# A written-out order of steps for linear attention with an expert layer, replaced by another one

## The chip, the cores and the metric

The kernel runs on one core of a Trainium2 chip. The metric is the device time of one execution in microseconds (us); the time given for a kernel is the median of its runs. The core has a matrix engine (PE, with PEld for its weight loads), a vector engine (DVE), a scalar engine (ACT), a general engine (POOL), and a queue (SP) that issues all transfers of this kernel. Each engine takes its instructions strictly in the order in which the program gave them, and waits where an operand is not there yet.

## The reference

The inputs are `q`, `k`, `v` with 8 batches, 8 heads, 576 rows and 64 columns, and the weights of a feed-forward layer. All are float32 or float64 as drawn; the feed-forward weights arrive as 64-bit words.

```python
q_s = softmax(q, axis=-1)              # over a head's 64 columns
k_s = softmax(k, axis=2)               # over the 576 rows
kv  = einsum('bhsd,bhse->bhde', k_s, v)
x   = einsum('bhsd,bhde->bhse', q_s, kv)     # -> 4608 x 512
h   = x @ w_in                         # 512 -> 1024
solu = h * softmax(h, axis=-1)
ln  = (solu - mean) / sqrt(var + 1e-06) * g_ln
out = ln @ w_out                       # 1024 -> 512, float32
```

## The kernel before

The 4608 rows are cut into 36 tiles of 128 rows: four tiles for each batch from its first 512 rows, and one for each pair of batches from the 64 rows that remain of each. The work is written as Python generators, one per piece of work, and each `yield` ends a step. The pieces are:

- `LK`, `LV`, `LQ`, `V` (batch number): transfers of keys, values, queries, and the copy of values into `vm` (L161 on ACT, L163 on DVE).
- `K` + batch: the softmax of the keys and their product with the values. DVE takes the largest over rows in parts (`khalf` L365, `ktop` L367 and L370), PE turns it (`turned` L341), DVE reduces it (`col` L344), PE spreads it (`wide` L348), ACT copies it (`kb` L351), POOL or DVE subtracts it (`km` L376, `kr` L381), ACT takes the exponential (L378, L383), and PE multiplies (`kv` L395, L400). The result goes, scaled, into `bd` (L422 to L426).
- `Q` + batch + a, b or c: the softmax of the queries (L443 largest, L445 subtraction, L447 exponential, L450 sum, L452, L454, L456 product, L161 or L163 cast into `qhl`, L461 the rest of the cast), and a transposing transfer (L484).
- `x` + tile: attention of one tile on PE (L529), brought into two float16 halves (`xT`, ACT L541, DVE L543).
- `h` + tile: 24 products of 512 columns into `h` (L566; the very first tile has 16 float32 ones, L558), and then the chain of the activation: largest (DVE L573), `nm` (ACT L575), exponential `e` (ACT L579), four small steps on POOL or DVE (L583, L586, L589, L592), the product (DVE L595), the mean `nmu` (ACT L597), two float16 halves `u` (ACT L600, DVE L602), a transposing transfer (L605), and the squares (ACT L609), which are the last to read `h`. There are two buffers for `h`, so that a tile's first product waits for the squares of the tile two places ahead of it.
- `o` + tile: 24 products into the output (L640), the eviction (ACT L650 or DVE L648), and the transfer out (L653).
- `w`, `W`, `y`, `Z`: loading and splitting of the two weight matrices; `S`: a scale; `R`: queries of the remaining rows; `P`: four warm-up products of no use (L696).

What sets the order is a string, `ORDER`. It names one piece after another; each name runs that piece up to its next `yield`. A suffix `.v` puts the step on DVE, where the step can choose its engine; without it the step goes to POOL or ACT, as the line says. `*2` repeats. So `ORDER` alone decides in which order each engine, and the transfer queue, gets its instructions, and which engine takes the optional ones:

```python
for item in order.split():
    item, _, times = item.partition("*")
    key, _, engine = item.partition(".")
    for _ in range(int(times or 1)):
        step(key, engine)
```

Of the kernel before, what the change touches and what calls it, by code (L numbers as in the profile page):

```python
# [23 lines left out]
    "LQ0*2 LK0 Q0a.v Q0a Q0b.v Q0a.v LK0 Q0c.v K0 LK0 w3 K0 w3 Q0c.v V00 K0 V03 Q0c.v Q0b K0 w0 P w0 "  # L24
    "Q0b.v w3 Q0a.v V00 K0 Q0b Q0a K0 K0.v Q0a K0 V03 V02.v K0 w3*2 Q0a.v LV0 V01 Q0b w0 K0.v P K0 V02 "
    "V01 P K0.v K0 w2 w0*2 Q0a K0.v K0 Q0b.v P K0 w0 Q0b K0 Q0c w2 K0 w2 K0 w1 w2 w1 LK1 K0*2 Q0b P K0 w2 "
    "Q0c w3 P w1*2 P K0*2 P K0*2 w1 w2 K0*2 w1 K1*2 x0 W LK1 x0 Q0c K1 W*2 h0 K1 V11 W V11 h0 K1 V12 y0 "
    "h0 Q0c.v W*4 h0.v W y0 W x1 y0 S0 K1 y1 W x1 y1 y0 h0.v V13.v K1 y1 y0 x1 LQ1 Q0c h0.v K1 h1 K1 h1.v "
    "h0 y1 y2 h1.v W LV2 V12 h0 h1.v x2 x3 y0 h0.v V13 y2 h0 h0.v h1 Q1a h0 h1.v K1 P V10 y1 y3 K1 x2 "
    "h0.v*2 Q1a x3 h0.v x2 Q1a h1 y2 K1 h1.v y1 K1 x3 h1.v*2 K1 h1 Q1a h2*2 V10.v h2 h1 Q1c K1 LG h2 "  # L30
    "Q1a*2 h1 h2*2 h1 LV1 y2 h2.v K1 h2.v K1 Q1a K1*2 h2 y3 P h2 Q1a.v y3 h1.v K1*2 LQ1 h1.v P h1.v y2 "
    "h2.v h2 K1 y2 Q1c h1 h3 K1*2 h2 y3 K1 h3*2 K1 h2 h3 y3 LK2 h3 K1 y3 K1 x5 h2 x4 h1.v Z x5*2 h2*2 h0 "
    "h0.v h0 h3.v h0.v Q1c.v Z*2 h1.v Z*2 h3 Z h5 Z h5 Z*2 o0.v Z h1 h2.v Z h5 Z*2 V22.v Z h2 Z LK2 h5.v "
    "h5 Z o0.v o0 h2 Z*3 h3*2 V21 o0 h3*3 LQ1 V22 Z o0 V21 Q1c o1 h5.v V23 o0 Q1c o1.v x4 S1 h3 R1.v R1 "
    "h3.v h5 h3 V23.v R1 h2.v K2 x4 o1.v o1*2 Q1c h3.v h3 h5*2 h4.v R1 K2 Q1c h4 V20.v Q1c.v h4.v K2 o0 "
    "h5 K2.v LQ2 h4 R1.v h3.v h5.v h3 h4 R1 K2 h5.v h4.v K2 o2 o1 h5.v o2.v o1.v h5.v K2.v*2 h4.v x6 x7 "
    "h5 h5.v K2.v x6 R1.v o2 h4.v h4 V32 h4.v h4 x6 h5 S1.v o2.v*2 R1 K2 h3.v K2 Q2a V20 K2.v h6.v h4 "
    "K2.v h4.v Q2c.v K2 h6 h6.v h6 h4.v h6 h6.v K2 h4.v h5.v x7 Q2a V33 K2.v o2 x8 Q2c h4 Q2a.v h6 K2 "
    "h4.v K2 x7 h7.v h3 h6.v Q2a h7 h6.v h4 K2.v Q2c h6.v h7.v h5 K2 Q2c Q2a LV3 o3.v V33 h7.v h5.v h6 "
    "h6.v o3.v h7 K2 K2.v Q2a h5 LK3 Q2a.v K2.v h4.v K2*2 K2.v h4 Q2c h7 K2 Q2a o3 K2.v h7 V32.v h7.v K3 "  # L40
    "h6.v o3 K3.v h6.v o3 h4.v o3.v K3 S2 o4.v x9 x10 h6.v o4 x9 S1 o4 K3 LK3 h7 x8 K3 h7 Q2c o4 h6.v "
    "h7.v*2 x9 o3 h6 x10 h6 h9 h7 K3 V31.v h7 K3.v h9.v*2 h7.v Q2c.v h9.v h7.v h9*2 o2 K3.v x10 h7.v K3 "
    "h6.v o4 h9 LQ3 h9 h10.v K3.v o5 h9.v h10 V30.v h9 Q2c.v h10.v h10 V31 h9.v LQ3 h9 h6 o4 h7 x8 h10 "
    "o5.v h6 h9.v h9*2 h10.v K3.v*2 h9 K3.v K3 h9.v o5 h7.v o5.v h10 Q3c o6 h10 h10.v h10 V30 h8.v K3.v "
    "h10.v Q3a o5.v h10 h10.v h8.v h7.v h8*2 K3.v Q3a LV4 Q3a.v o5.v K3 h10.v Q3c.v Q3a h10.v h10 x11 K3 "
    "x12 LK4 h8 x11 x12 h7 Q3a*2 x11 K3 h8 LQ3 o6.v h8 V41.v h8.v K3 h8 h8.v h10 K3 K3.v V43 h8 h8.v K3.v "
# [47 lines left out]
    "o33 h35*2 o31 o27 h35.v o28.v o27.v h34*2 o27*4 h34.v h35.v h34.v h34 h34.v o31 h35 h34 h35.v o30.v "  # L94
    "h34 o31 o33 o27 o30 o30.v*2 h34 o32.v o33 h35 o30.v o33 h35.v h35 o32 o28.v h35.v o30.v o31.v o32.v "
    "h35.v o32 h35 o31 h35 o32 h35 o32 h35 h35.v o32.v h35 h35.v o34 o35 o33 o34 o33 o34 o33.v o34 o34.v "
    "o34 o34.v o35.v*3 o35*2 o35.v*2 o35*5 "
)


# [660 lines left out]
```

## Time and profile before

| what | value |
|---|---|
| time, median of 3 runs | 473.68 us (472.71 to 475.24) |
| the profiled execution, its own time | 472.75 us |
| its span, first to last instruction | 471.0 us |
| PE busy | 443.1 us, 94% of the span |
| DVE, ACT, POOL busy | 350.5, 285.5, 196.1 us |

The page of the profile shows one execution. The share of an engine's busy time is an average over the whole span; the beginning, where weights and the first keys are loaded and prepared, differs from the long middle, where PE always has a tile to work on. A row of the trace gives start, duration (both in us), engine, line, operation, output <- input, and in brackets how long the engine stood idle ahead of it and what ended that.

### The profile page before, as it was taken

The page shows a single profiled execution, that of the slowest core. Times are in us where ns is not written, and L with a number is a line of the kernel's source. Part 1 is how long each engine was busy: PE and PEld are TensorE (multiplying, and loading weights), DVE is VectorE, ACT ScalarE, POOL GpSimd, SP SyncE. Part 2 cuts the span into 40 slices and gives each one's busy share as a digit, 9 for nine tenths or more (in the row PEclk, how much of TensorE's full clock was granted, in tenths as well). Part 3 has the DMA queues.
Part 4 walks back from the last instruction along what each step waited for, and adds up shares of the span by engine and source line. Part 5 has one row for each costly group of instructions (what it writes and reads, how often), then busy time and mean ns, then how long its engine had stood idle before and what let it go on. Part 6 is the DMA issues. An engine that isn't in the chain of part 4 may idle for free.

```text
span 471.0 us, 8293 instructions
## 1 busy us (share of the span) xinstructions
PE 443.1 (94%) x3142; PEld 221.2 (47%) x3142; DVE 350.5 (74%) x602; ACT 285.5 (61%) x473; POOL 196.1 (42%) x300
## 2 busy tenths in 40 slices
PE   1678989998999999999999999999999999999997
PEld 0333444455545444544454455444445444444444
DVE  4989999989989887788998888875856755554030
ACT  2688999668657674757576557644566545431231
POOL 4122974665434194941255357412353431221100
PEclk9989999999999999999999999999999999999999
DMA  8999968696695958299859944797222462515141
GB/s 271 267 273 344 244 143 200 131 236 162 125 211 116 250 133 226 73 209 216 191 150 208 227 101 81 167 276 169 69 67 53 106 134 47 123 34 111 47 129 49
DMA packets 159240, 74.99 MB, mean 159 GB/s; under 512 B 127840, under 2 KB 152672, under 8 KB 159200
## 3 DMA queue, kind: packets, MB, share of 16 engines
q1 hardware_dynamic: 159200, 74.47, 67.1%
q8 instruction: 24, 0.39, 0.3%
q14 instruction: 16, 0.13, 0.1%
HBM read 36.70 MB, written 9.44 MB: 98 GB/s over the span
## 4 chain that ended last, share of the span: by engine, by line
PE 68%; DVE 18%; DMA 5%; issue 3%; ACT 3%; POOL 1%; SPq 1%; DVEq 0%; ACTq 0%; POOLq 0%
PE o L640 32%; PE h L566 30%; PE kv L395 3%; DMA qm<-in_q_dram 2%; PE x L529 2%; DVE h L595 2%; DMA km<-in_k_dram 2%; DVE u L602 2%; DVE top L573 2%; DVE khalf L365 1%; DVE qnmx L443 1%; DVE wo L330 1%; DVE qsum L450 1%; DMA kr<-in_k_dram 1%; PE kv L400 1%
## 5 line engine op out<-in xcount | busy, mean ns | idle before, releaser
L640 PE MATMUL o<-wo,uT 128*128 128x512 f16 (+1 forms) x888 | 198.3, 373 | 0.3 <-ACT os L650 0.2
L566 PE MATMUL h<-wi,xT 128*128 128x512 f16 x840 | 194.0, 379 | 4.7 <-ACT e L609 4.0
L640 PEld LDWEIGHTS <-uT 128*128 128x128 f16 x888 | 86.1, 98 | 97.1 <-issue 0.7
L566 PEld LDWEIGHTS <-xT 128*128 128x128 f16 x840 | 81.6, 98 | 102.3 <-issue 5.7
L573 DVE TENSOR_REDUCE top<-h 128x1 f32<-128x1024 f32 x36 | 43.9, 1221 | 21.5 <-PE h L566 21.3
L602 DVE SCALAR_TENSOR_TENSOR u<-h,nmu,u 128x1024 f16<-128x1024 f32 x36 | 46.0, 1277 | 15.6 <-ACT u L600 15.5
L595 DVE SCALAR_TENSOR_TENSOR h<-h,ph,e 128x1024 f32<-128x1024 f32 x36 | 46.3, 1285 | 11.7 <-POOL ph L592 9.8
L609 ACT ACTIVATE e<-h,nmu 128x1024 f32<-128x1024 f32 x36 | 40.1, 1113 | 18.5 <-DVE u L602 18.4
L456 POOL TENSOR_TENSOR qm<-qm,qrec 128x1024 f32<-128x1024 f32 (+1 forms) x15 | 27.4, 1825 | 39.2 <-DVE qrec L454 30.8
L600 ACT ACTIVATE u<-h,nmu 128x1024 f16<-128x1024 f32 x36 | 40.0, 1112 | 1.0
L589 POOL TENSOR_TENSOR p<-pi,mone 128x1 f32<-128x1 f32 x36 | 24.2, 672 | 36.1 <-DVE pi L586 34.6
L579 ACT ACTIVATE e<-h,nm,hs 128x1024 f32<-128x1024 f32 x31 | 37.3, 1202 | 0.7
L597 ACT ACTIVATE nmu<-s 128x1 f32<-128x1 f32 x36 | 7.3, 202 | 46.2 <-DVE h L595 45.9
L575 ACT ACTIVATE nm<-top,hs 128x1 f32<-128x1 f32 x31 | 9.1, 293 | 40.5 <-DVE top L573 40.4
L650 ACT ACTIVATE os<-o,rr 128x512 f32<-128x512 f32 (+1 forms) x24 | 16.0, 665 | 26.3 <-PE o L640 23.7
L583 POOL TENSOR_SCALAR am<-nm 128x1 f32<-128x1 f32 x19 | 9.0, 471 | 50.0 <-ACT nm L575 49.9
L622 POOL TENSOR_TENSOR r<-var,mhalf 128x1 f32<-128x1 f32 x36 | 21.6, 599 | 17.1 <-DVE var L619 15.2
L543 DVE SCALAR_TENSOR_TENSOR xT<-x,xT 128x512 f16<-128x512 f32 x35 | 23.8, 681 | 2.4 <-ACT xT L541 2.4
L443 DVE TENSOR_REDUCE qnmx<-qm 128x16 f32<-128x1024 f32 (+1 forms) x17 | 19.4, 1149 | 6.9 <-DMA qm<-in_q_dram 6.9
L447 ACT ACTIVATE qm<-qm 128x1024 f32<-128x1024 f32 (+1 forms) x17 | 17.0, 1005 | 11.7 <-POOL qm L445 7.7
L541 ACT ACTIVATE xT<-x 128x512 f16<-128x512 f32 x35 | 20.0, 594 | 6.5 <-PE x L529 6.5
L376 POOL TENSOR_TENSOR km<-km,kb 128x1024 f32<-128x1024 f32 x8 | 18.9, 2360 | 6.4 <-ACT kb L351 6.3
(138 smaller groups left out, 556.9 us busy)
## 6 DMA issues: line engine op xcount, KB each, us to landing
v<-in_v_dram SPq DMA_DIRECT2D x32, 256.0 KB, 4.1
out_dram<-os SPq DMA_DIRECT2D x31, 256.0 KB, 3.3
km<-in_k_dram SPq DMA_DIRECT2D x7, 1024.0 KB, 6.5
qm<-in_q_dram SPq DMA_DIRECT2D x7, 1024.0 KB, 7.0
w_in<-in_moe_w_in_dram SPq DMA_DIRECT2D x8, 512.0 KB, 7.1
w_out<-in_moe_w_out_dram SPq DMA_DIRECT2D x8, 512.0 KB, 4.9
out_dram<-os SPq DMA_DIRECT2D x10, 128.0 KB, 2.4
qm<-in_q_dram SPq DMA_DIRECT2D x2, 512.0 KB, 4.3
```

Source lines behind the costliest of these rows:

```text
L443: nc.vector.tensor_reduce(shaped(nmx), x, axis=AX.X, op=ALU.max, negate=True)
L456: on(nc.gpsimd).tensor_tensor(x, x, wide(rec), op=ALU.mult)
L543: nc.vector.scalar_tensor_tensor(xT[:, 1], acc, 1.0 / QS, xT[:, 0], op0=ALU.mult, op1=ALU.subtract)
L566: nc.tensor.matmul(h[:, ns], xT[:, t, kc], wi[:, s, kc, ns], start=(i == 0), stop=(i == len(terms) - 1))
L573: nc.vector.tensor_reduce(top, h, axis=AX.X, op=ALU.max, negate=True)
L579: nc.scalar.activation(e, h, AF.Exp, bias=nm, scale=hs, accum_out=z)
L589: nc.gpsimd.tensor_tensor(p, pi, mone, op=ALU.pow)
L595: nc.vector.scalar_tensor_tensor(h, h, ph, e, op0=ALU.mult, op1=ALU.mult, accum_out=s1)
L600: nc.scalar.activation(u[:, 0], h, AF.Identity, bias=nmu)
L602: nc.vector.scalar_tensor_tensor(u[:, 1], h, nmu, u[:, 0], op0=ALU.add, op1=ALU.subtract)
L609: nc.scalar.activation(e, h, AF.Square, bias=nmu, accum_out=s2)
L640: nc.tensor.matmul(o, uT[:, j, f], wo[:, s, f, cols], start=(f == 0 and j == 0 and s == 0), stop=(f == NF - 1 and j == 1))
```

## The change

Only the string `ORDER` is another one. It has the same 1725 steps, each as often as before, among them 11 warm-up steps `P`; the steps stand in another order, and other ones of them have the suffix `.v`. Its first line before and after:

```diff
-    "LQ0*2 LK0 Q0a.v Q0a Q0b.v Q0a.v LK0 Q0c.v K0 LK0 w3 K0 w3 Q0c.v V00 K0 V03 Q0c.v Q0b K0 w0 P w0 "
+    "LQ0*2 Q0a*2 LK0*3 Q0b.v Q0c.v Q0a.v Q0b V03 K0.v w3 Q0a w3 K0 Q0a.v Q0a K0*2 Q0b V03 Q0c.v*2 V00 w0 "
```

PE gets the same number of products. DVE's program goes from 564 to 583 rows, ACT's from 392 to 388, POOL's from 305 to 291. The sequence in which tiles enter their `h` products is the same. Three places of the new order, as each engine's program has it:

DVE at the very beginning, where the keys of batch 0 (`ktop`, `col`) and its queries (`qm`, `qhl`) are prepared, before:

```order
L450 TENSOR_REDUCE qsum_0_140<-qm_97 128x8
L452 TENSOR_SCALAR qden_0_142<-qsum_0_140 128x8
L454 RECIPROCAL qrec_0_144<-qden_0_142 128x8
L370 TENSOR_TENSOR ktop_111<-ktop_111,kr_114 64x512
L450 TENSOR_REDUCE qsum_1_148<-qm_97 128x8
L452 TENSOR_SCALAR qden_1_150<-qsum_1_148 128x8
L454 RECIPROCAL qrec_1_152<-qden_1_150 128x8
L344 TENSOR_REDUCE col_160<-turned_155 128x4
L260 TENSOR_SCALAR iw_138<-iw_138 128x1024
L262 SCALAR_TENSOR_TENSOR iw_138<-w_in_116,iw_138 128x1024
L461 TENSOR_TENSOR qhl_0_162<-qm_97,qhl_0_162 128x8x64
```

The same place now:

```order
L454 RECIPROCAL qrec_0_125<-qden_0_123 128x8
L367 TENSOR_TENSOR ktop_116<-khalf_117 128x256
L456 TENSOR_TENSOR qm_97<-qm_97,qrec_0_125 128x8x64
L365 TENSOR_TENSOR khalf_117<-km_103 128x512
L367 TENSOR_TENSOR ktop_116<-khalf_117 128x256
L445 TENSOR_TENSOR qm_97<-qm_97,qnmx_2_110 128x8x128
L370 TENSOR_TENSOR ktop_116<-ktop_116,kr_106 64x512
L450 TENSOR_REDUCE qsum_1_145<-qm_97 128x8
L452 TENSOR_SCALAR qden_1_147<-qsum_1_145 128x8
L454 RECIPROCAL qrec_1_149<-qden_1_147 128x8
L461 TENSOR_TENSOR qhl_0_130<-qm_97,qhl_0_130 128x8x64
L344 TENSOR_REDUCE col_158<-turned_151 128x4
```

The product L456 has come to DVE from POOL and stands ahead of L370; L461 stands ahead of `col` and no longer behind it.

ACT at the chain of tile 1 (`nmu_1`, `u_1`, and its squares in the last row), with tile 2's exponential in between, before:

```order
L161 CAST qhl_0_614<-qm_439 128x8x2x64
L597 ACTIVATE nmu_1_618<-s_1_616 128x1
L600 ACTIVATE u_1_628<-h_1_451,nmu_1_618 128x1024
L575 ACTIVATE nm_2_634<-top_2_632,hs_413 128x1
L579 ACTIVATE e_2_653,z_2_654<-h_2_589,nm_2_634,hs_413 128x1024
L258 ACTIVATE gw_701<-w_out_547 128x1024
L609 ACTIVATE e_1_569,s_1_716<-h_1_451,nmu_1_618 128x1024
```

The same place now:

```order
L597 ACTIVATE nmu_1_631<-s_1_629 128x1
L161 CAST qhl_0_633<-qm_472 128x8x2x64
L575 ACTIVATE nm_2_637<-top_2_635,hs_403 128x1
L600 ACTIVATE u_1_641<-h_1_507,nmu_1_631 128x1024
L579 ACTIVATE e_2_643,z_2_644<-h_2_570,nm_2_637,hs_403 128x1024
L258 ACTIVATE gw_713<-w_out_611 128x1024
L609 ACTIVATE e_1_588,s_1_720<-h_1_507,nmu_1_631 128x1024
```

The cast of the queries and the small L575, which waits for tile 2's largest value, have moved between tile 1's mean and its `u`.

DVE at the chain of tile 4 (batch 1's first tile, `h_0`), where the keys of batch 2 are prepared too, before:

```order
L602 SCALAR_TENSOR_TENSOR u_1_1103<-h_1_856,nmu_1_1093,u_1_1103 128x1024
L461 TENSOR_TENSOR qhlr_1073<-qr_707,qhlr_1073 128x8x64
L586 TENSOR_SCALAR pi_0_1171<-am_0_1167 128x1
L543 SCALAR_TENSOR_TENSOR xT_2_1155<-x_2_1116,xT_2_1155 128x512
L509 COPY hsr_1178<-hs_413 64x1
L619 TENSOR_SCALAR var_3_1068<-s_3_1018,z_3_1064 128x1
L443 TENSOR_REDUCE qnmx_0_1197<-qm_1055 128x16
L381 TENSOR_TENSOR kr_889<-kr_889,kb_1153 64x512
L595 SCALAR_TENSOR_TENSOR h_0_1025,s_0_1209<-h_0_1025,ph_0_1206,e_0_1164 128x1024
L443 TENSOR_REDUCE qnmx_2_1213<-qm_1055 128x16
L602 SCALAR_TENSOR_TENSOR u_0_1228<-h_0_1025,nmu_0_1211,u_0_1228 128x1024
```

The same place now:

```order
L602 SCALAR_TENSOR_TENSOR u_1_1068<-h_1_868,nmu_1_1058,u_1_1068 128x1024
L376 TENSOR_TENSOR km_775<-km_775,kb_1127 128x1024
L543 SCALAR_TENSOR_TENSOR xT_2_1166<-x_2_1132,xT_2_1166 128x512
L595 SCALAR_TENSOR_TENSOR h_0_1041,s_0_1205<-h_0_1041,ph_0_1179,e_0_1099 128x1024
L443 TENSOR_REDUCE qnmx_0_1233<-qm_1092 128x16
L443 TENSOR_REDUCE qnmx_2_1235<-qm_1092 128x16
L602 SCALAR_TENSOR_TENSOR u_0_1209<-h_0_1041,nmu_0_1207,u_0_1209 128x1024
```

Ahead of L595 the subtraction of the keys `kr` (L381) has gone to POOL, one of `km` (L376) has come from there, and the queries' L443 stands behind it. On PE the attention of the remaining rows, `x_4`, which stood between the two halves of batch 2's `kv` products, now comes after tile 3's output.

146 rows, old and new, of the table ORDER are left out of this document.

## The prediction

> **What bounds the kernel now.** I read the page first, for who is busy.
>
> ```profile
> span 471.0 us, 8293 instructions
> PE 443.1 (94%) x3142; PEld 221.2 (47%) x3142; DVE 350.5 (74%) x602; ACT 285.5 (61%) x473; POOL 196.1 (42%) x300
> ```
>
> PE has work for 443.1 of 471.0 us, and the change takes no product away from it. All that another order can win is in the other 27.9 us, and it can lose without a limit. So the next view is the busy time by stretches of 20 us (columns: PE, PEld, DVE, ACT, POOL, granted PE clock, share of the DMA engines, GB/s), for where those 27.9 us are.
>
> ```profile
> 0.00:20.00 20.00, 7.15 (x20) 3.12 (x21) 13.70 (x25) 8.43 (x12) 7.75 (x13) 1.00 0.87 280
> 20.00:40.00 20.00, 15.91 (x132) 7.76 (x131) 17.53 (x36) 17.06 (x25) 3.76 (x3) 0.91 1.08 290
> 100.00:120.00 20.00, 18.64 (x185) 10.01 (x183) 18.16 (x33) 13.98 (x24) 14.72 (x15) 1.00 0.82 173
> 280.00:300.00 20.00, 20.00 (x208) 11.11 (x207) 17.68 (x29) 13.02 (x22) 12.84 (x18) 1.00 0.53 114
> ```
>
> The first 40 us lack 16.9 us of PE work, the stretch from 100 another 1.4, and a stretch in the middle nothing. The kernel is therefore a beginning that is bound by loads, DVE and ACT, and then PE alone. The third view is what PE waited for (us in total, times, longest).
>
> ```profile
> PE turned L341 <- DVE ktop L370: 10.3, 1, 10.3
> PE h L566 <- ACT e L609: 4.0, 5, 1.4
> ...
> PE x L529 <- DMA qTr<-qhlr: 0.4, 1, 0.4
> ```
>
> The 10.3 us are the first keys; nothing can run ahead of them. The 4.0 us are the two `h` buffers: PE waits until ACT's squares (L609) let one go. That is the wait which the order of DVE and ACT governs, and it falls at few places, shown below. The end is PE alone:
>
> ```profile
> 433.59 33.89 PE L640 MATMUL o<-wo,uT 128*128 128x512 f16 x180
> ```
>
> **The change part by part.** The same pieces run on PE, so every term is a wait made or saved. I take four places.
>
> *The first keys.* DVE and PE before:
>
> ```profile
> 13.12 0.63 DVE L370 TENSOR_TENSOR ktop<-ktop,kr 64x512 f32<-64x512 f32 x1
> ...
> 15.02 0.69 DVE L344 TENSOR_REDUCE col<-turned 128x4 f32<-128x512 f32 x1
> ...
> 17.83 0.68 DVE L461 TENSOR_TENSOR qhl<-qm,qhl 128x512 f16<-128x512 f32 x1
> 18.44 1.22 DVE L376 TENSOR_TENSOR km<-km,kb 128x1024 f32<-128x1024 f32 x1
> ```
>
> The next keys' first DVE row, which waits for its load:
>
> ```profile
> 33.69 0.69 DVE L365 TENSOR_TENSOR khalf<-km 128x512 f32<-128x512 f32 x1 [0.97 <-DMA km<-in_k_dram]
> ```
>
> Ahead of L370 there is now one more L456 of 128 x 512 on DVE. This form ran on DVE once, on the remaining queries, in 683 ns:
>
> ```profile
> L456 DVE TENSOR_TENSOR qr<-qr,qrecr x1: 683/683/683, 91.3 to 91.3; 128x512 f32<-128x512 f32 x1
> ```
>
> So L370 and with it PE's first useful work come 0.68 us later. L461 (0.68) now stands ahead of `col`, which makes `col` 1.3 us later, but it no longer stands between `col` and L376: at L376 the lateness is 0.68 again, and 0.0 to 1.3 are its bounds (none, if DVE had to wait there for `kb` anyway; all, if `kb` now comes last). What comes after: the exponentials, the first `kv`, then the next load of `km`, whose buffer becomes free by that `kv`, then `khalf`, which waits 0.97 for this load, then the first `h`:
>
> ```profile
> 27.82 5.73 PE L696 MATMUL warm_up<-bd 128*128 128x512 f16 x16
> 33.49 0.64 PE L529 MATMUL x<-qT,bd 128*64 128x128 f16 x16
> 34.96 0.32 PE L173 MATMUL wide_in<-ident,m_in 128*128 128x128 f32 x1 [0.83 <-DVE m_in L279]
> 35.12 7.03 PE L558 MATMUL h<-iw,xT 128*128 128x512 f32 x16
> ```
>
> I take **+0.5**, near the 0.68, because the chain goes through that load; the range is 0 to 1.3. Four warm-ups now stand between `x` and `wide_in`, where PE waited 0.83; a quarter of 5.73 is 1.4 at that pace, so they cost nothing to 0.6, inside this range. `col` of the next keys and `x_1` change places; PE waits there for `h`'s chain in any case.
>
> *Tile 1's squares.* ACT before, and the PE row that waits for it:
>
> ```profile
> 60.13 1.03 ACT L161 CAST qhl<-qm 128x1024 f16<-128x1024 f32 x1
> 61.06 0.20 ACT L597 ACTIVATE nmu<-s 128x1 f32<-128x1 f32 x1
> 61.29 1.11 ACT L600 ACTIVATE u<-h,nmu 128x1024 f16<-128x1024 f32 x1
> ...
> 64.85 1.10 ACT L609 ACTIVATE e<-h,nmu 128x1024 f32<-128x1024 f32 x1
> ```
>
> ```profile
> 66.09 4.48 PE L566 MATMUL h<-wi,xT 128*128 128x512 f16 x20 [1.40 <-ACT e L609]
> ```
>
> The cast (1.03) filled ACT's time ahead of the mean (0.20, at 61.06). Now the mean comes first, but `u` has the cast and the small step for tile 2's largest value ahead of it. If the mean can start at its sum's end, about 0.5 earlier, `u` starts at 60.6 + 0.2 + 1.03 and some tenths for the small step, near 62.0 and not at 61.29: 0.7 to 0.85 later, all of which goes on to L609, behind which PE stands. The lower bound is 0: what is late at the beginning is late here as well, and is not paid twice. I take **+0.5**. Queued behind L609 on ACT is only weight preparation; behind the PE row is everything.
>
> *Tile 4's squares and `x_4`.* DVE, POOL, ACT and PE before:
>
> ```profile
> 100.77 1.22 DVE L443 TENSOR_REDUCE qnmx<-qm 128x16 f32<-128x1024 f32 x1 [1.72 <-DMA qm<-in_q_dram]
> 101.90 2.35 DVE L381 TENSOR_TENSOR kr<-kr,kb 64x512 f32<-64x512 f32 x1
> 104.19 1.28 DVE L595 SCALAR_TENSOR_TENSOR h<-h,ph,e 128x1024 f32<-128x1024 f32 x1
> ```
>
> ```profile
> 101.36 2.36 POOL L376 TENSOR_TENSOR km<-km,kb 128x1024 f32<-128x1024 f32 x1
> ```
>
> ```profile
> 107.93 0.70 PE L529 MATMUL x<-qTr,bd 128*64 128x64 f16 x32 [0.37 <-DMA qTr<-qhlr]
> ...
> 111.20 2.75 PE L566 MATMUL h<-wi,xT 128*128 128x512 f16 x12 [0.99 <-ACT e L609]
> ```
>
> L595 stood behind a reduction that waited 1.72 for queries, and behind a `kr` of 2.35 us. Both are gone from ahead of it, and one `km` of 1.22 (the row at 18.44) has come: up to 1.72 + 1.22 + 2.35 - 1.22 = 4.1 us earlier, less what DVE then waits for `kb`. PE can win no more than its two waits, 0.37 + 0.99 = 1.36, and gives back that `x_4` (0.70) no longer fills part of this time. Bounds: -1.4 and +0.7. I take **-0.9**, nearer to the first, because the wait's cause is moved by more than its length.
>
> The 2.35 us of L381 have a reason that weighs here. It began while POOL's `km` ran (101.36 to 103.72) and ended 0.53 after it. [...]
>
> *The rest.* Of PE's 4.0 us of waits for L609, little lies after 112 us; this is the same view of PE's waits for the stretch from there to the end, and then two pieces from the chain of waits (start, us, what):
>
> ```profile
> PE h L566 <- ACT e L609: 0.2, 1, 0.2
> ```
>
> ```profile
> 297.46 5.18 PE h L566 x24
> ...
> 311.72 1.02 PE h L566 x4
> ```
>
> It is 0.2 us. 24 products take 5.18 us. Between tile 24's end, 297.46 + 5.18 = 302.64, and the next use of its buffer, 311.72, stand 42 products, 9.1 us, and that was just enough. In the new order there are 60 at this place, but at tile 14 it goes from 85 products' worth to 48, 10.5 us, and at tile 22 from 84 to 48. All are over 9.1. So the middle should not become slower: **-0.4** for the small waits after 112 us, 0.2 at L609 and some tenths at transposed keys, with bounds -0.8 and +1.5 (the most that I give to three such tight tiles at half a us). The larger operations moved between DVE and POOL balance: four L445 leave DVE, three long L456 and two short ones come, three L461 leave. DVE is at 74%, so this costs nothing while PE is the bound; where DVE is full, up to 120 us, it is in the terms above. At the end, 33.89 us of PE with no gap, the last eviction follows the last product in both orders: 0.
>
> **The sum.** +0.5 + 0.5 - 0.9 - 0.4 = -0.3 on the profiled execution's 472.75 (471.0 of span and 1.75 around it), so 472.45. That execution is near the fastest of the runs (472.71 to 475.24); their median, 473.68, is 0.93 above it. With this added: **473.4 us**.
>
> **The rivals.** *Faster:* the new order removes the `h` waits altogether, 4.0 and 0.4 for the transposed queries, and loses nothing at the beginning: 472.75 - 4.4 + 0.93 = 469.3. For it: those waits sit on ACT and DVE, where the order is rewritten. Against it: at the first three tiles the same operations stand ahead of L595 as before; only their order differs.
>
> *Slower:* DVE's queue at the beginning is what decides. `col` is 1.3 us late in full, because L456 and L461 are ahead of it; the second half of tile 1's `xT` has two weight operations more ahead of it and makes `h_1` end about 0.9 later, and the cast adds 0.85: 472.75 + 1.3 + 0.9 + 0.85 + 0.93 = 476.7. It decides from the point at which `kb`, and not DVE, is last to come ahead of L376. For it: DVE and ACT are over 17 of 20 us from 20 to 40. Against it: DVE waited 0.97 for `km` in that stretch, which takes up some lateness.
>
> *The clock:* the granted clock is 0.91 from 20 to 40 us, and 16 warm-ups that need 3.46 at the 0.216 of the row with 24 took 5.73. The loss fell on products of no use. If it falls on the first `h` (7.03 us) instead, the clock that is lost in that stretch, (1 - 0.91) x 20 = 1.8 us, is on the path: 473.4 + 1.8 = 475.2. The new place of four warm-ups, directly ahead of that `h`, speaks against it. [...]
>
> *That nothing changes:* as PE's products and the tiles' order are the same, it may be a reshuffle inside slack; that is my forecast's neighbour, 473.7.
>
> **How the numbers follow.** Forecast, with the reshuffle, 0.52; faster 0.27; slower by DVE's queue 0.14; the clock 0.07. About 0.5%, 2.4 us here, is what a measurement of this kernel can tell from no change: 471.3 to 476.05. The faster case lies below, the slower one above, the clock case mostly within, with a tail above when it meets the late `col`. So faster 0.27, within 0.54, slower 0.19. The range reaches to the faster case and a little past the slower one, 469.2 to 477.0; the forecast's own goes from all terms at their lower bounds (0 + 0 - 1.4 - 0.8, or 471.5) to half way towards all at the upper ones (1.3 + 0.85 + 0.7 + 1.5, or 478.0), 475.7.
>
> **What would show it.** L370 near 13.8 and `col` near 16.3 show the first term, L558 between 35.2 and 36.4 its sum. PE's wait ahead of the `h` with 20 products near 66 us should be over 1.4 for the second term. L595 of tile 4 before 103 and a wait under 0.5 ahead of the `h` near 110 show the third. PE waits for L609 of over 1 us in total after 112 us, or a last stretch of PE with gaps, would make the prediction wrong, and so would a first `h` before 34.5.

## The result and the profile after

The changed kernel takes 468.61 us (median of 4 runs, 468.31 to 468.78), the kernel before 473.32 us beside it (4 runs, 472.71 to 475.24). The ratio is 0.9897, with a 95% interval of 0.987 to 0.9925. The prediction said 473.4 us and no change; the change made the kernel 4.7 us faster, and the time lies below the predicted range. A second comparison with more runs, told below, gave 469.29 against 473.3, ratio 0.9914 (0.9896 to 0.9933); that time lies just inside the range's lower end of 469.2.

The head of the profiled execution's page:

```profile
span 467.0 us, 8294 instructions
PE 439.9 (94%) x3142; PEld 221.4 (47%) x3142; DVE 349.9 (75%) x620; ACT 282.4 (60%) x469; POOL 200.0 (43%) x286
```

The span is 4.0 us shorter with the same 3142 products. Only 0.8 us of this is idle time of PE as the profile counts it (27.9 us before, 27.1 now); the busy time of PE fell too, by 3.2 us. The stretches that the prediction showed, now (columns as there):

```profile
20.00:40.00 20.00, 17.33 (x137) 8.51 (x136) 17.91 (x36) 17.30 (x26) 4.16 (x3) 0.91 1.07 323
100.00:120.00 20.00, 20.00 (x178) 10.32 (x178) 18.44 (x34) 16.11 (x27) 15.23 (x17) 1.00 0.80 176
```

From 100 to 120 us PE now has no gap (20.00 and not 18.64). From 20 to 40 it is busier as well (17.33 and not 15.91), but with four more warm-up products. What PE waited for (us in total, times, longest):

```profile
PE turned L341 <- DVE ktop L370: 14.4, 1, 14.4
PE kv L173 <- DVE mx L409: 2.8, 2, 1.4
PE h L566 <- ACT e L609: 2.3, 3, 1.5
PE wide L348 <- DVE col L344: 2.3, 2, 1.2
PE kv L395 <- ACT km L378: 1.1, 1, 1.1
PE h L566 <- DVE xT L543: 0.5, 1, 0.5
```

The first wait is longer by 4.1 us, for two reasons: four warm-ups that stood ahead of it, until 3.62 us, come later now, and `turned` itself starts 0.50 us later (14.40 and not 13.90). The waits for L609 fell from 4.0 to 2.3, the last of which ends at 73 us. The wait for `qTr` is gone, and so are three small ones that stood late in the kernel. After 74 us the view names no wait of PE at all.

**Where the 4.0 us come from.** All kernels here run the same products on PE, and two rows stand in every trace: the `h` in one run of 24 products near 101 us (tile 6), and the last 168 products of the output. In the kernel before (PE):

```profile
101.14 5.34 PE L566 MATMUL h<-wi,xT 128*128 128x512 f16 x24
```

Its last stretch of 180 products starts at 433.59 (in the prediction's row), and 12 products of 0.216 us later, at 436.18, come the last 168. In the changed kernel:

```profile
101.23 5.34 PE L566 MATMUL h<-wi,xT 128*128 128x512 f16 x24
...
432.19 31.30 PE L640 MATMUL o<-wo,uT 128*128 128x512 f16 x168
```

From the first of these places to the second the kernel before takes 436.18 - 101.14 = 335.04 us, the changed one 432.19 - 101.23 = 330.96, so **4.08 us less**. Up to the first place it takes 0.09 us more. I call the 335.04 the *body* and what lies ahead of it the *beginning*. All of the traced gain is in the body. When the starts of equal products are compared along it, 1.7 us are won from 105 to 112 us and 2.4 us after that, in small steps.

### The profile page after: what moved, and what is told of

Its sections match the earlier page's. It is cut to its first block, busy times and chain, and to the rows that moved or that the text cites. A ratio compares the mean times of both kernels' runs of the same rounds, so it can differ in the third digit from the quotient of the medians.

```text
span 467.0 us, 8294 instructions
## 1 busy us (share of the span) xinstructions
PE 439.9 (94%) x3142; PEld 221.4 (47%) x3142; DVE 349.9 (75%) x620; ACT 282.4 (60%) x469; POOL 200.0 (43%) x286
## 4 chain that ended last, share of the span: by engine, by line
PE 86%; DVE 6%; POOL 3%; ACT 3%; DMA 1%; issue 1%; SPq 0%; POOLq 0%; ACTq 0%; DVEq 0%
PE o L640 40%; PE h L566 36%; PE x L529 3%; PE kv L395 3%; PE warm_up L696 1%; DMA qm<-in_q_dram 1%; PE kv L400 1%; DVE wi L289 1%; DVE qnmx L443 1%; POOL qm L445 1%; PE turned L341 1%; PE wide L348 1%; DVE iw L262 1%; POOL km L376 1%; DVE km L376 0%
## 5 line engine op out<-in xcount | busy, mean ns | idle before, releaser
L609 ACT ACTIVATE e<-h,nmu 128x1024 f32<-128x1024 f32 x36 | 40.1, 1113 | 22.1 <-DVE u L602 22.1
L595 DVE SCALAR_TENSOR_TENSOR h<-h,ph,e 128x1024 f32<-128x1024 f32 x36 | 46.3, 1287 | 5.5 <-POOL ph L592 4.0
L589 POOL TENSOR_TENSOR p<-pi,mone 128x1 f32<-128x1 f32 x36 | 25.9, 718 | 49.5 <-DVE pi L586 42.7
L600 ACT ACTIVATE u<-h,nmu 128x1024 f16<-128x1024 f32 x36 | 40.0, 1112 | 0.8
L579 ACT ACTIVATE e<-h,nm,hs 128x1024 f32<-128x1024 f32 x31 | 37.2, 1201 | 0.7
L597 ACT ACTIVATE nmu<-s 128x1 f32<-128x1 f32 x36 | 7.3, 202 | 49.4 <-DVE h L595 49.3
L445 POOL TENSOR_TENSOR qm<-qm,qnmx 128x1024 f32<-128x1024 f32 (+1 forms) x14 | 25.7, 1844 | 21.7 <-DVE qnmx L443 14.6
L622 POOL TENSOR_TENSOR r<-var,mhalf 128x1 f32<-128x1 f32 x36 | 24.2, 675 | 22.5 <-DVE var L619 22.0
L461 POOL TENSOR_TENSOR qhl<-qm,qhl 128x1024 f16<-128x1024 f32 (+1 forms) x11 | 22.5, 2041 | 19.4 <-DVE qhl L163 10.3
L575 ACT ACTIVATE nm<-top,hs 128x1 f32<-128x1 f32 x31 | 9.1, 294 | 35.2 <-DVE top L573 35.0
L456 POOL TENSOR_TENSOR qm<-qm,qrec 128x1024 f32<-128x1024 f32 (+1 forms) x11 | 20.7, 1879 | 19.2 <-DVE qrec L454 19.1
L586 POOL TENSOR_SCALAR pi<-am 128x1 f32<-128x1 f32 x19 | 7.5, 393 | 41.8 <-DVE am L583 41.1
L443 DVE TENSOR_REDUCE qnmx<-qm 128x16 f32<-128x1024 f32 (+1 forms) x17 | 19.3, 1147 | 6.0 <-DMA qm<-in_q_dram 6.0
```

What stands on the lines that cost most here:

```text
L443: nc.vector.tensor_reduce(shaped(nmx), x, axis=AX.X, op=ALU.max, negate=True)
L445: on(nc.gpsimd).tensor_tensor(x, x, wide(nmx), op=ALU.add)
L579: nc.scalar.activation(e, h, AF.Exp, bias=nm, scale=hs, accum_out=z)
L589: nc.gpsimd.tensor_tensor(p, pi, mone, op=ALU.pow)
L595: nc.vector.scalar_tensor_tensor(h, h, ph, e, op0=ALU.mult, op1=ALU.mult, accum_out=s1)
L600: nc.scalar.activation(u[:, 0], h, AF.Identity, bias=nmu)
```

## The experiments

The order is a list of some 1700 steps; a key such as `h4` stands for the next piece of tile 4's product, `K2` for the next piece of batch 2's keys, and `.v` puts a step on VectorE (DVE; ScalarE is ACT and GpSimd is POOL). Gains in the body are read from the two PE places above, since they repeat much better than whole times. A number with a sign is the difference to the kernel before. A ratio is worked out from all runs of both kernels and can differ a little from that of the two medians.

| what | median us | ratio to before (95%) | `h` of tile 6 starts | body | body's difference |
|---|---|---|---|---|---|
| before, profiled | 473.2 to 473.3 | 1 | 101.14 | 335.04 | |
| changed, profiled | 468.61 | 0.9897 (0.987 to 0.9925) | 101.23 | 330.96 | -4.08 |
| changed, once more | 469.29 | 0.9914 (0.9896 to 0.9933) | 101.36 | 330.96 | -4.08 |
| changed beginning alone | 473.03 | 0.9986 (0.9968 to 1.0004) | 102.34 | 334.81 | -0.23 |
| changed middle alone | 472.86 | 0.9983 (0.9967 to 1.0) | 100.99 | 334.80 | -0.24 |
| changed from tile 6 on | 470.05 | 0.9909 (0.988 to 0.9939) | 104.20 | 330.96 | -4.08 |
| changed from tile 15 on | 480.2 | 1.0136 (1.0101 to 1.0171) | 103.93 | 342.44 | +7.40 |
| `x_4` moved | 474.8 | 1.0036 (1.002 to 1.0053) | 101.85 | 336.37 | +1.33 |
| L595 first on VectorE | 472.44 | 0.998 (0.9966 to 0.9994) | 101.59 | 334.17 | -0.87 |
| tile 4's place as changed | 471.75 | 0.9972 (0.9954 to 0.999) | 102.73 | 333.28 | -1.76 |
| three PE pieces | 472.32 | 0.9979 (0.9963 to 0.9995) | 103.15 | 334.14 | -0.90 |
| four PE pieces | 472.11 | 0.9984 (0.9964 to 1.0004) | 102.13 | 334.13 | -0.91 |
| tile 4's place and four PE pieces | 470.49 | 0.995 (0.9932 to 0.9967) | 101.58 | 332.33 | -2.71 |
| changed, eight warm-ups fewer | 469.02 | 0.9917 (0.9889 to 0.9944) | 101.49 | 330.96 | -4.08 |

The body of the changed order measures 330.96 us in four executions of three kernels. The order of before was traced once, so a difference to its body compares one trace with one. The beginning does not repeat: with before's order of the beginning, tile 6 starts between 100.99 and 104.20 us.

### The order by stretches

Four kernels take one stretch from one list and the rest from the other; steps already done are left out where the lists join. The changed beginning alone:

```diff
-all steps in the order of before
+the changed order up to the first h6, then the steps not yet done in the order of before
```

> The changed order up to the first piece of the product h of tile 6 (about 98 us), the order of before from there on. Theory 'place by place': the order is worth in each stretch what the two traces show at equal PE work, and the stretches are independent; up to 98 us the two traces differ by 0.1 us, so this kernel is within 0.4 us of before (473.0 to 473.7 with before at 473.3). Rival 'first terms': the lateness of 0.5 at the first keys and 0.5 at tile 1's squares is there, and something else in the head pays for it only in the later order: +0.5 to +1.0. Rival 'spread': the 0.7 us by which the median difference (4.7) exceeds that of the two traced spans (4.0) comes from the order of the beginning: -0.7.

Measured: 473.03 us, ratio 0.9986 (0.9968 to 1.0004), so between -1.5 and +0.2 us. The rival "first terms", +0.5 to +1.0, falls. Between the other two the interval doesn't decide. The body, in the order of before from tile 6 on, is within 0.23 us of before's.

The changed middle alone:

```diff
-all steps in the order of before
+the order of before up to some 20 steps ahead of the first h6, the changed order up to the first h9,
+then the steps not yet done in the order of before
```

> The order of before up to about 97 us, the changed order up to the first piece of h of tile 9 (about 125 us), the order of before from there on. 'Place by place': the two waits of PE near 108 and 111 us go, -1.8 us (471.5 with before at 473.3). Rival 'it is passed on': the small waits after 112 us are there because tile 4 was late, so that this piece of the order alone brings the whole -4 (469.3). Rival 'the blocked km': with kr on GpSimd the km on VectorE is blocked, so that the piece brings nothing (473.3).

Measured: 472.86 us. By equal work the trace won 1.8 us up to 124 us, as the first theory said, and gave 1.5 back from there to 160 us. Two rows with their waits after the join:

```profile
126.61 0.63 PE L341 MATMUL turned<-ident,ktop 128*128 128x128 f32 x4 [0.69 <-DVE ktop L370]
...
142.82 1.02 PE L566 MATMUL h<-wi,xT 128*128 128x512 f16 x4 [0.47 <-ACT e L609]
```

Neither wait is in the kernel before or in the changed one: they belong to the join, where steps that only one list has done early come late or in a heap. So the median tells little about the middle, and "it is passed on" and "the blocked km" are refuted only by the trace: the place itself won its 1.8 us, and the later stalls of before (at 177, 224, 311, 337 and 396 us, told below) are all still there.

The changed order from tile 6 on:

```diff
-all steps in the order of before
+the order of before up to some 20 steps ahead of the first h6, then the steps not yet done in the changed order
```

> The order of before up to about 97 us, the changed order from there to the end. 'Place by place': all of the difference of the two spans, -4.0 us (469.3 with before at 473.3). Rival 'first terms': 0.5 to 1.0 more than that, since the lateness of the beginning is left out: -4.5 to -5.0. Rival 'spread': -4.0 as well, but with runs that lie 2 us apart, as those of before do, and a median 0.7 above the changed kernel's.

Measured: 470.05 us, ratio 0.9909, so -4.3 us with an interval of -5.7 to -2.9; the body is 330.96, as in the changed kernel, to the hundredth. The whole gain of the body comes with the order from tile 6 on. The runs lie 2.8 us apart (468.88 to 471.72), as the third rival had it; the median is 1.44 above the changed kernel's first one (468.61) and 0.76 above its later one (469.29).

The changed order from tile 15 on:

```diff
-all steps in the order of before
+the order of before up to the first h15, then the steps not yet done in the changed order
```

> The order of before up to the first piece of h of tile 15 (about 203 us), the changed order from there to the end. 'Place by place': at equal work the traces drift apart by 1.8 to 2.0 us after that point, in steps at 223, 337 and 395 us, so -1.9 (471.4 with before at 473.3). Rival 'it is passed on' (late stalls follow from a late tile 4): near 0, within 0.5 us of before. Rival 'it is passed on, in full': -4.

Measured: 480.2 us, which no theory had. PE and ACT in its trace:

```profile
219.57 3.57 PE L566 MATMUL h<-wi,xT 128*128 128x512 f16 x8 [6.08 <-ACT e L609]
```

```profile
214.27 1.04 ACT L161 CAST qhl<-qm 128x1024 f16<-128x1024 f32 x1 [8.79 <-issue]
```

At the join a cast of queries came to stand on ACT ahead of tile 14's small steps and did not start for 8.79 us; the profile names no releaser. The buffer that it writes was still being read by a transposition that had been issued just before, so this is the likely reason, but it is argued and not shown. Behind this wait PE was also granted less clock, 0.52 on average from 218 to 225 us, and the eight products above took 3.57 us, where the eight at 116.05 us in the kernel before took 1.89. After the join the kernel won 1.1 us more, as the changed one does there. This kernel tells of its join and not of the change; lists of this kind can't be cut anywhere. The next experiments therefore move single steps.

### The changed kernel once more

```diff
 the changed kernel, unaltered
```

> The changed kernel once more. Question: is the 4.7 us by which its median lay under that of before the order's, or is 0.7 of it the executions' own spread? Theory 'order plus beginning': the part after 105 us is the order's and the same in every execution (-4.0 us at equal PE work), the part before that is a matter of when the first loads of keys land (8.5 to 10 us in the four profiles of the first experiments) and varies by 1 to 3 us in both kernels; then the runs spread over 2 us here too, and the median is 4.0 to 4.7 under before's (468.6 to 469.3). Rival 'robust beginning': the runs again lie within 0.6 us, and 4.7 or more under before's median.

Measured: 469.29 us (468.41 to 470.33, 6 runs), 4.0 below before's 473.3. The runs are 1.9 us apart, so it was chance that the four runs of the first comparison lay within 0.5 us, and the rival "robust beginning" falls. What differs from execution to execution lies in the beginning. The first keys don't always land at the same time. VectorE's first row on them, in the kernel before and then in the kernel of the join at tile 15, whose first 200 us have the same order:

```profile
8.47 1.04 DVE L365 TENSOR_TENSOR khalf<-km 128x512 f32<-128x512 f32 x1
```

```profile
9.96 0.69 DVE L365 TENSOR_TENSOR khalf<-km 128x512 f32<-128x512 f32 x1 [1.44 <-DMA km<-in_k_dram]
```

But this does not order the beginnings: in the trace whose tile 6 starts last (104.20) this row starts at 8.49, and in the one whose tile 6 starts first (100.99) at 9.38. PE's clock orders them better. There are stretches in which it is granted half its clock. In the kernel before it is granted 0.50 from 27.6 to 31.0 us, 3.4 us long, and this falls on warm-ups. In the trace of the three moved pieces (told below), which begins in the same order, another one falls on needed products. The view by stretches (columns as in the prediction) and PE:

```profile
67.00:70.00 3.00, 3.00 (x8) 1.06 (x7) 3.00 (x5) 2.89 (x7) 2.81 (x3) 0.50 1.00 196
```

```profile
66.61 6.16 PE L566 MATMUL h<-wi,xT 128*128 128x512 f16 x20 [1.42 <-ACT e L609]
```

The same 20 products took 4.48 us in the kernel before (the prediction's row at 66.09). In the trace with `x_4` moved the slow stretch (clock 0.50 from 36 to 38 us) falls on the first `h`, which took 7.03 us before:

```profile
34.58 8.73 PE L558 MATMUL h<-iw,xT 128*128 128x512 f32 x16
```

Of the ten profiles that begin in before's order, six have such a stretch on needed products ahead of tile 6, at 1.6 to 1.7 us each: in these six tile 6 starts at 101.85 to 104.20 us, in the other four at 100.99 to 101.59. From the start of the first `h` to that of tile 6 the six take 67.15 to 68.23 us, the four 65.67 to 66.02. In the three profiles that begin in the changed order no needed product met it; whether that order avoids it, or three executions are too few to meet it, is not shown. One of the three starts tile 6 at 102.34 all the same, so the clock is not the only cause.

### `x_4` alone

```diff
-o2 x8 Q2c
+o2 Q2c
...
-o3.v K3 S2
+o3.v x8 K3 S2
```

(`x8` is the key of the tile whose product is named `x_4`.)

> Before, with the 32 products of x_4 alone moved on PE, from between the halves of batch 2's kv to behind the last product of tile 3's output. Theory 'one chain': the h behind it waits for tile 4's squares, which end at the same time as before, so the h starts no earlier, PE only waits longer ahead of it, and x_4's own 0.7 us come on top: +0.7 (bounds 0 and +0.8) at equal PE work after 130 us. Rival 'two waits': each wait of PE is a loss of its own, and the 0.37 us (0.59 with what the record hides) for the turned queries go: -0.4 to -0.6.

Measured: 474.8 us, +1.33 in the body. PE:

```profile
111.89 2.75 PE L566 MATMUL h<-wi,xT 128*128 128x512 f16 x12 [1.52 <-ACT e L609]
...
124.05 1.08 PE L529 MATMUL x<-qT,bd 128*64 128x128 f16 x32 [0.90 <-DMA qT<-qhl]
```

"One chain" is right in its sign and its mechanism: the wait for L609 grew from 0.99 to 1.52 as `x_4` left, the `h` started no earlier (10.04 us after tile 6, and 10.06 before), and `x_4`'s own products came on top, +0.45 at equal work. The other 0.9 is a new wait, for the transposed queries of the next products, whose landing took 6.1 us after its issue instead of 4.5; why is not shown. The rival "two waits" falls: the wait for `qTr` of 0.37 us in the kernel before cost nothing, for PE stood ahead of the same L609 anyway.

### VectorE's order at tile 4 alone

```diff
-K2 Q2a V20 K2.v h6.v h4 K2.v h4.v Q2c.v
+K2 V20 h6.v h4 h4.v K2.v K2.v Q2a Q2c.v
```

> Before, with VectorE's order changed at one place alone: the sum with the product of tile 4 (L595) goes ahead of the subtraction kr (L381) and of the reduction that waits for queries (L443); no step changes its engine. Theory: L595 starts near 101.4 instead of 104.2, L609 ends near 107.5 instead of 111.0, and the 1.2 us of PE ahead of the next h go, less up to 0.4 because kr and the second part of the keys are later: -0.8 to -1.2 at equal PE work after 112 us. Rival 'the kr matters': only the move of kr to GpSimd brings the gain, and the later kr delays the kv: 0 or slower, up to +0.5. Rival 'two chains': L595 comes early but ScalarE's queue holds L609 back: -0.3 to 0.

Measured: -0.87 in the body, 0.77 of it at this place; 472.44 us. (On ACT the small `nmu`, L597, moves with L595, ahead of `kr`'s exponential.) L595 started at 101.89. ACT, and PE behind it:

```profile
104.74 0.63 ACT L383 ACTIVATE kr<-kr 64x512 f32<-64x512 f32 x1 [1.27 <-DVE kr L381]
105.28 1.09 ACT L600 ACTIVATE u<-h,nmu 128x1024 f16<-128x1024 f32 x1
...
109.64 1.09 ACT L609 ACTIVATE e<-h,nmu 128x1024 f32<-128x1024 f32 x1
```

```profile
110.88 2.75 PE L566 MATMUL h<-wi,xT 128*128 128x512 f16 x12 [0.78 <-ACT e L609]
```

`u` (L600) stands behind `kr`'s exponential on ACT, and that waits 1.27 us for the `kr` which now comes after L595 on VectorE. So "two chains" names what is left, and the gain lies at the lower end of the theory's range.

### Tile 4's place as in the change

```diff
-K2 h3.v K2 Q2a V20 K2.v h6.v h4 K2.v h4.v Q2c.v
+K2.v h3.v K2 V20 K2 h6.v h4 K2.v h4.v Q2a Q2c.v
```

The first `km` goes to VectorE, `kr` to GpSimd, L443 behind L595; PE's order, with `x_4` in its old place, stays.

> Before, with tile 4's place on VectorE and GpSimd alone as in the change: the first km of batch 2 on VectorE, kr on GpSimd in its place, and the reduction that waits for queries (L443) behind L595. PE's order, x_4 and all else stay. Theory: L595 starts near 100.4 instead of 104.2, kr's exponential no longer stands ahead of u on ScalarE, L609 ends before PE comes: -1.2 to -1.6 at equal PE work from 105 to 130 us. [...] Rival 'ScalarE's queue', as the run before showed: -0.8.

Measured: 471.75 us, -1.76 in the body (-1.6 up to 115 us). VectorE, then GpSimd, in its trace:

```profile
100.44 1.21 DVE L376 TENSOR_TENSOR km<-km,kb 128x1024 f32<-128x1024 f32 x1
...
102.97 1.29 DVE L595 SCALAR_TENSOR_TENSOR h<-h,ph,e 128x1024 f32<-128x1024 f32 x1 [1.19 <-POOL ph L592]
```

```profile
100.49 2.29 POOL L381 TENSOR_TENSOR kr<-kr,kb 64x512 f32<-64x512 f32 x1
```

```profile
111.17 1.04 PE L566 MATMUL h<-wi,xT 128*128 128x512 f16 x4
```

The `h` of tile 7 no longer waits, and a stall of 0.2 us at 123 us is gone too. The swap between the two engines, not the later `x_4`, makes the gain at this place. The rival "the blocked km" of the changed middle took `km` on VectorE to be the one that is held up. Here `km` took 1.21 us, and it was `kr` on GpSimd that took 2.29: it began 0.05 us after VectorE's `km` and ended 1.13 us after it. In the changed kernel the two didn't meet, and it took 1.27 (GpSimd):

```profile
99.95 1.27 POOL L381 TENSOR_TENSOR kr<-kr,kb 64x512 f32<-64x512 f32 x1
```

But the longer `kr` cost only the 1.19 us for which L595 waited here (for `ph`, which stands behind `kr` on GpSimd), and with this wait L595 was early enough.

### Three and four pieces on PE alone

Three pieces, each moved by one or two places on PE; no other engine's order changes:

```diff
-h9 K4 h12 h13.v h13.v
+h9 h12 h13.v K4 h13.v
...
-h25.v h26 K7 h28 Q7a x29 h25 K7 h25 o21
+h25.v o21 h26 K7 h28 Q7a x29 h25 K7 h25
...
-o29 h31 h32 h32
+h31 h32 o29 h32
```

> Before, with three pieces moved on PE alone, each by one or two places: the transposed keys of batch 4 (at 224 us, where PE waited for VectorE's xT) behind one more piece of h, one output piece ahead of the h that waited for L609 at 337 us, one output piece at 396 us behind one more piece of h. Theory 'small and local': the stalls are 0.57, 0.37 and 0.36 us by the starts of the products, though the view of waits shows only 0.41, 0.21 and 0.20; each goes by itself and nothing comes back: -0.8 to -1.3 at equal PE work from 112 us to the end. Rival 'as the view says': -0.8 at the most, since 0.82 is all that the view has there. Rival 'passed on': the stalls come back at the next tile: -0.3 to 0.

The expectation put the first piece at the wrong place: by the trace, the transposed keys that were moved are those at 177 us, not those at 224, and their stall was 0.17 us and named nowhere in the view. So the theory's sum was 0.17 + 0.37 + 0.36 = 0.90. Measured: -0.90 in the body, taken off at 177, 337 and 396 us in just these steps, and nothing came back; 472.32 us. Of PE's waits from 118 us to the end the view then names only

```profile
PE turned L341 <- DVE xT L543: 0.4, 1, 0.4
```

The view had shown 0.21 + 0.20 = 0.41 us for what was worth 0.90. The kernel before at 337 us shows why (PE):

```profile
336.17 1.03 PE L566 MATMUL h<-wi,xT 128*128 128x512 f16 x4
337.40 1.02 PE L566 MATMUL h<-wi,xT 128*128 128x512 f16 x4 [0.21 <-ACT e L609]
```

Four products take 4 x 0.216 = 0.86 us from start to start, so the next could have started at 337.03. It started at 337.40: 0.37 us were lost. The row's 1.03 ends at 337.20, since a product's record (0.379 us on average) is 0.16 us longer than the step to the next product, and the view counts only from there. Every stall behind such a product is 0.16 us too short in the view, and those of 0.17 us at 177 and 0.18 at 311 aren't in it at all.

The fourth piece:

```diff
-K5.v x19 h17
+x19 h17 K5.v
```

> Before, with four pieces moved on PE alone: the three of the earlier run (which, by its trace, took away the stalls at 177, 337 and 396 us; the piece of batch 4 is the one at 177, not the one at 224) and the transposed keys of batch 5 at 224 us behind one more piece of h. Theory 'small and local': -0.90 again for the three and -0.4 to -0.6 for the fourth, -1.3 to -1.5 at equal PE work from 112 us on. Rival: the fourth is only shifted, since the h behind it waits for L609 until nearly the same time: -0.9 to -1.1.

Measured: -0.91 in the body, so the fourth piece brought nothing. PE:

```profile
224.68 1.02 PE L566 MATMUL h<-wi,xT 128*128 128x512 f16 x4 [0.17 <-ACT e L609]
...
230.73 1.46 PE L640 MATMUL o<-wo,uT 128*128 128x512 f16 x6
232.28 1.02 PE L566 MATMUL h<-wi,xT 128*128 128x512 f16 x4
```

The `h` that went ahead waits for L609, and a later one starts 0.25 us late (230.73 + 6 x 0.216 = 232.03). As the rival said, this stall was only shifted. It went in the changed kernel, whose DVE and ACT are ordered otherwise there.

All five places together:

```diff
-K2 h3.v K2 Q2a V20 K2.v h6.v h4 K2.v h4.v Q2c.v
+K2.v h3.v K2 V20 K2 h6.v h4 K2.v h4.v Q2a Q2c.v
...
 and the four pieces above
```

> Before, with tile 4's place on VectorE and GpSimd as in the change and the four pieces on PE: five places of some 1700 steps. Theory: the stalls are separate, the gains add up, -2.5 to -3.1 at equal PE work, median 470.2 to 470.8 with before at 473.3. Rival 'the whole order': such gains are only to be had with the order as a whole, and single moves give them back: -1.5 or less.

Measured: 470.49 us, ratio 0.995 (0.9932 to 0.9967); the body is 2.71 shorter, against 1.76 + 0.91 = 2.67 for its parts. The gains add up. "The whole order" falls as far as two thirds of the gain are concerned. For the last 1.4 us no single move is shown: the fourth piece only shifted its stall, and others were not tried.

### Eight warm-ups fewer

```diff
-P (the last of the four ahead of x_0)
-P (the one between x_0 and wide_in)
```

> The changed kernel with eight warm-up products fewer: the last four of the 16 ahead of x_0 and the four between x_0 and wide_in are gone (work that no output needs). Theory 'warm-ups set the first h': in the changed kernel's trace x_0 starts at the end of the warm-ups (33.45), while bd is ready at 32.8 and the copy of x_0 follows it; so the first h starts 0.3 to 0.6 us earlier, and the lateness of the first keys, which the prediction priced at 0.5, had been covered by these products: -0.3 to -0.6 against the changed kernel (468.7 to 469.0 with its 469.3). Rival 'clock': without them the stretch at half clock falls on the first h: +0.5 to +2. Rival 'swallowed': h starts earlier and the waits for L609 at the next tiles take it up: within 0.2.

Measured: 469.02 us against 469.29 for the changed kernel, within both intervals, so the time doesn't decide. The trace does, in part (PE):

```profile
27.76 5.75 PE L696 MATMUL warm_up<-bd 128*128 128x512 f16 x12
33.44 0.64 PE L529 MATMUL x<-qT,bd 128*64 128x128 f16 x16
...
34.77 7.13 PE L558 MATMUL h<-iw,xT 128*128 128x512 f32 x16 [0.44 <-ACT xT L167]
```

12 warm-ups took as long as 16 did (5.67 in the changed kernel's trace), as a longer part of them ran at half clock (the granted clock from 28 to 32 us is 0.50 here and 0.64 there): `x_0` started no earlier. The first `h` began 0.23 us earlier than in the changed kernel's profile, because `wide_in` had four products fewer ahead of it, and here it waited for ACT. So the first theory fails in its first step in this trace: fewer warm-ups did not make `x_0` start earlier. But one trace of each kernel can't show what eight warm-ups do, for in the second profile of the changed kernel, whose granted clock is 0.999 on average (0.996 in the first), its 16 took 4.27 us:

```profile
28.55 4.27 PE L696 MATMUL warm_up<-bd 128*128 128x512 f16 x16
```

Here the half clock did not reach the first `h` (7.13 us, 7.03 before), but it did reach products of a later one, at 65.76 us, whose 20 took 5.35 us and not 4.48 (the granted clock from 50 to 70 us is 0.91). No version is shown to beat the changed kernel.

## Why the prediction was wrong

**The first keys, +0.5: the chain was right, the price was not.** VectorE in the changed kernel:

```profile
13.57 0.68 DVE L370 TENSOR_TENSOR ktop<-ktop,kr 64x512 f32<-64x512 f32 x1
...
15.77 0.68 DVE L344 TENSOR_REDUCE col<-turned 128x4 f32<-128x512 f32 x1
...
18.47 1.22 DVE L376 TENSOR_TENSOR km<-km,kb 128x1024 f32<-128x1024 f32 x1
```

L370 came 0.45 later (predicted 0.68) and `col` 0.75 (predicted 1.3), but L376 only 0.03. The step that failed is "at L376 the lateness is 0.68 again". That the way from `col` to L376 gets shorter by L461 was right (2.70 us now, 3.42 before, so 0.72 less); but the two operations put ahead of `col` had made it only 0.75 late and not 1.3, so that nothing was left. The first `h` began at 35.00 and not at 35.12, under the 35.2 that was named as the term's sign. One trace can't measure 0.5 us there, though: the ten profiles that begin in before's order have this row between 34.58 and 36.75. The run with the changed beginning alone excludes +1.0 for the first two terms together.

**Tile 1's squares, +0.5: what was moved ahead of `u` had stood ahead of L609 before.** ACT in the changed kernel:

```profile
60.26 0.18 ACT L597 ACTIVATE nmu<-s 128x1 f32<-128x1 f32 x1
60.61 1.05 ACT L161 CAST qhl<-qm 128x1024 f16<-128x1024 f32 x1 [0.17 <-POOL qm L456]
61.57 0.29 ACT L575 ACTIVATE nm<-top,hs 128x1 f32<-128x1 f32 x1
61.76 1.09 ACT L600 ACTIVATE u<-h,nmu 128x1024 f16<-128x1024 f32 x1
62.76 1.19 ACT L579 ACTIVATE e<-h,nm,hs 128x1024 f32<-128x1024 f32 x1
...
63.94 1.14 ACT L258 ACTIVATE gw<-w_out 128x1024 f32<-128x1024 f32 x1
64.97 1.11 ACT L609 ACTIVATE e<-h,nmu 128x1024 f32<-128x1024 f32 x1
```

In the kernel before the small L575 came behind `u` and not ahead of it:

```profile
62.31 0.28 ACT L575 ACTIVATE nm<-top,hs 128x1 f32<-128x1 f32 x1
```

`u` is 0.47 late, near what was said (61.76 for "near 62.0"). But "all of which goes on to L609" is wrong. The same six operations stand ahead of L609 in both orders: the cast, the mean, `u`, L575, the exponential L579 and the weight preparation L258. ACT goes through them almost without a pause, in 4.72 us before (60.13 to 64.85) and in 4.71 now (60.26 to 64.97), so what `u` loses by L575 ahead of it is won back behind it. L609 is 0.12 late, no more than the first of the six (0.13). PE's next `h` began 0.14 later. Its wait of 0.37, and not over 1.4, says nothing of this term, since all eight warm-ups of that place now stand right ahead of it.

**Tile 4's squares and `x_4`, -0.9: right cause, too small, and wrong on `x_4`.** VectorE, then PE, in the changed kernel:

```profile
100.09 1.28 DVE L595 SCALAR_TENSOR_TENSOR h<-h,ph,e 128x1024 f32<-128x1024 f32 x1
```

```profile
109.14 4.49 PE L566 MATMUL h<-wi,xT 128*128 128x512 f16 x20
```

L595 came at 100.09 (predicted: before 103), the wait ahead of tile 7's `h` is gone, and 1.7 us were won. The bound of 1.36 was read from two waits in the view, 0.37 and 0.99, which are 0.56 and 1.06 by the starts of the products (the `h` starts 1.21 after the start of the last `kv` product, and such a change takes 0.15 in the changed kernel), 1.62 together; the run with this place alone won 1.6 here. And `x_4`'s 0.70 was booked as a price, while the two runs show that its place matters only for as long as L609 is late: the swap without it brings 1.76 in the body, the move without the swap costs 1.33 (0.45 here, the rest at the new wait). The longer `kr` that the prediction saw on VectorE beside GpSimd's `km` (2.35 us) has its counterpart in the runs: `kr` on GpSimd took 1.27 us in the changed kernel, where the two did not meet, and 2.29 beside VectorE's `km`. In the run where they met, `km` took 1.21 us, and the 1.19 us for which L595 then waited were less than the slack that the swap makes.

**The rest, -0.4: this step failed, and it is half of the error.** It measured -2.4. The prediction took its 0.2 us from the wait view and added "some tenths", and the view hides 0.16 us of each stall. Start to start, the body of before has six stalls after 112 us, at 123, 177, 224, 311, 337 and 396: 0.21 + 0.17 + 0.57 + 0.18 + 0.37 + 0.36 = 1.86 us, where the view has 0.82. The changed kernel has none of them. Three were taken away by three pieces moved on PE, for 0.90, and the one at 123 went with tile 4's place; the one at 224 was only shifted, and that at 311 was not tried. It is the place that the prediction called just enough: 0.18 us were lost there. The remaining 0.5 us are for the most part a second thing that the prediction didn't count: a change of PE between 128*128, 128*64 and 64*64 products (the sizes behind the names in the rows) costs mostly 0.09 to 0.12 us more than the usual step, start to start. After 112 us there are 29 of these instead of 32, since three changes from 64*64 products of `kv` to `x` are gone, some 0.36 us; what is left are steps of under 0.1 us. That was read from the starts and not tested by itself.

With this falls the premise that all that another order can win is in the 27.9 us in which PE is not busy. The body in the view by stretches, before and then in the changed kernel:

```profile
101.14:436.18 335.04, 332.70 (x2407) 166.13 (x2406) 257.65 (x437) 199.39 (x336) 141.37 (x231) 1.00 0.65 145
```

```profile
101.23:432.19 330.96, 330.96 (x2407) 166.18 (x2406) 253.43 (x454) 195.03 (x331) 146.06 (x212) 1.00 0.66 145
```

PE counts as idle for 2.34 us before and for none now; the other 1.74 of the 4.08 us were won inside what counts as busy.

The tight places named there (48 products where 42 had been 0.18 us too few) held, as predicted: no wait for L609 after 74 us.

**The tail, 0:** right; the last stretch has no gap in either order.

**The 0.93 from the profiled run to the median:** it was right for the kernel before. Its profiled execution is one of the four in which no needed product met the slow stretch. In the ten profiles that begin in its order, tile 6 starts at 100.99 to 104.20 us, with a median of 102.0, which is 0.85 after the profiled 101.14. It did not hold for the changed kernel, whose median was 0.15 below its profiled run at first and 0.41 above it later. Three profiles that begin in its order have 101.23, 101.36 and 102.34. Whether its beginning is earlier on average (the run of the beginning alone gives -0.7 with an interval of -1.5 to +0.2) stays open, and with it whether the median gained 4.1 us or up to 0.6 more.

**The sum:** -3.7 us of error in the span's sum (-0.3 against -4.0) are 0.5 from the first keys, 0.4 from tile 1, 0.8 from tile 4 and 2.0 from the rest.

**The rivals.** *Faster* came nearest with 469.3, but partly by chance: it took away all waits for L609, 4.0 us, of which 2.3 remained, and the small stalls made up the difference. *Slower* fell, since `kb` was not last ahead of L376. *The clock:* what it describes does occur, at the price that it named: in two of the ten profiles that begin in before's order the half-clock stretch fell on the first `h` (8.73 us and not 7.03, so 1.70), and in four on a later one. In the changed kernel's two profiles it met no needed product, so it did not make that one slower. *Nothing changes* fell.

## What to carry to other kernels

When one engine has work for 94% of the span and only the order changes, count what it loses from the starts of its instructions against their usual step, not from the view of waits: here the view had 0.82 us after 112 us, the starts 1.86. A stall is worth its length only if the wait behind it does not end at the same event: moving `x_4` out of its wait cost 1.33 us, while removing the wait of both, on other engines, won 1.76. And measure a stage between two places that every trace has: the body of the changed order repeats to 0.01 us in four traces, while the whole time varies by up to 5 us, with its beginning, so edits of a few tenths of a us can be read there. Where a stage does not repeat, compare the granted clock of several executions before giving another cause.

## What the hardware showed that was not expected

The stage from tile 6 to the last products took 330.96 us in four executions, although their beginnings were 3 us apart (101.23 to 104.20). `kr` took longer beside the other engine's `km`, on either engine: VectorE's `kr` took 2.35 us beside GpSimd's `km` (and ended 0.53 us after it) and 0.68 at 19.57 us in the same trace; GpSimd's `kr` took 2.29 beside VectorE's `km`, and 1.27 where the two did not meet. PE's granted clock was 0.50 for 3.4 us (27.6 to 31.0) in the kernel before, on warm-ups; in the same order of steps such a stretch met the first `h` in another execution (8.73 us and not 7.03) and a later `h`, at 67 us, in a third (6.16 and not 4.48). The first load of keys was used by VectorE between 8.47 and 9.96 us, in the same order of steps.
